# A list scheduler that places relus and output copies itself, counts no latency within an engine, and knows measured load times

## Chip, cores, metric

One core of one Trainium2 chip. The metric is the device time of one execution in microseconds; executions of one kernel mostly agree within 0.3%. The kernel before takes 317.23 us (median of 4 runs, 316.78 to 317.42).

## The reference, cut to what matters

```python
# q, k, v: (4, 8, 768, 64); blocks of 32; mask = neighbours, first and last block, 3 sampled blocks per row block
scores = np.where(mask, scale * np.matmul(q, k.transpose(0, 1, 3, 2)), -1e9)
attn = softmax(scores);  o = np.matmul(attn, v)
x = o.transpose(0, 2, 1, 3).reshape(3072, 512)
h = np.maximum(x @ w_in, 0.0)          # (3072, 2048)
out = (h * h) @ w_out                  # (3072, 512)
```

## The kernel before

While the kernel is built, a list scheduler simulates the five engines with planned durations and emits each task's instructions in the order that it finds. The chip then runs every engine's queue strictly in that order, with semaphores between engines. So the plan decides the order and nothing else; the real times are the chip's.

```python
def ready(self, taken, bufs):                 # earliest planned start of a task
    r = self.after
    for d in self.deps:
        r = max(r, d.end + d.late)            # late: 0.2 us for TensorE's results, 0.08 for VectorE's and ScalarE's
    ...                                       # and the buffers: ps 2, po 1, h 2, y 1 in PSUM
def run_schedule(free, bufs, ring):
    left = {e: [t for t in tasks if t.eng == e] for e in free}
    ...                                       # task that can start first, then smallest key
# --- cut ---
def relu_eng(T, f):                           # fixed: one third, or one half, of the relus on ScalarE
    return "ACT" if (T[0] and f % 3 == 2) or (T[0] == 0 and T[1] and f % 2) else "DVE"
def out_copy(T, ts): ...; nc.scalar.copy(out=ys, in_=py)     # always ScalarE
# --- cut ---
h0, hh = [Task("PE", SQ[w][0] / 2, n_key - half, ...) for half in range(2)]   # hidden product ph: two halves
land_k = [(3.05, 4.3), (5.6,), (8.3,), (11.0,)]              # planned landing of the four head pairs' keys
wu = [Task("PE", 0.107, 1e6, warm_up, ...) for i in range(16)]   # fillers, besides ten at the start
```

TensorE's products are called after what they write: pw warm-ups, pt transposes, pb and pq the mask's products, ps scores, po values (weights times v and row sums), ph hidden, py output. ScalarE makes pT (exponentials) and the inverse of the row sums (ls twice, then rs); VectorE multiplies by the mask and normalises into xT; GpSimd squares.

The softmax here doesn't subtract the row's maximum and nothing guards it: scores larger than these inputs give would overflow.

## Time and profile before

The profiled run took 316.91 us, with a span of 315.2 us in the profile. The prediction shows the profile's lines and sums TensorE's ledger: the distance between starts of successive matmuls, split into the pace of the matmul, 0.096 us for a passage between 64-row or 24-row and 128-row matmuls, and the rest, called a wait. Single waits over 60 ns are put down to what released them. In the first 3.7 us the rest also holds the slow pace of the first warm-ups, some 1.1 us.

### The profile page before, as it was taken

To read this page: it belongs to the slowest core of one execution; us is meant where nothing else is said; L and a number is where in the kernel's file an instruction comes from. 1 tells how busy PE (TensorE), PEld (TensorE's weight loads), DVE (VectorE), ACT (ScalarE), POOL (GpSimd) and SP (SyncE) were. 2 spreads that over 40 slices of the span, in tenths; PEclk is the share of its full clock that TensorE was granted. 3 is DMA by queue.
4 is the path that set the end of the run, shared out by engine and by line. 5 is a ranking of instruction groups with operands and counts; after the bars stand their busy time and mean duration, and the time that the engine had idled before them with its cause. 6 is when DMAs were issued, how large, how long until landed. Compare 5 with 4: busy or idle time off the path is not lost.

```text
span 315.2 us, 6102 instructions
## 1 busy us (share of the span) xinstructions
PE 304.4 (97%) x2303; PEld 171.9 (55%) x2303; DVE 211.2 (67%) x378; ACT 227.3 (72%) x364; POOL 179.2 (57%) x224
## 2 busy tenths in 40 slices
PE   6899999999999989999999999999999999999995
PEld 3565554556656534565565655565555555555542
DVE  7526399785966978979976679776787676332200
ACT  3799999666878999779868888879787886311111
POOL 5560297556875815887756449654544335465620
PEclk9999999999999999999999999999999999999999
DMA  7997369507438355257361075420000000000002
GB/s 223 344 191 150 114 102 199 169 35 200 113 122 235 62 199 177 58 177 196 81 191 35 30 207 128 131 60 33 2 33 35 0 36 34 35 33 33 35 33 100
DMA packets 42597, 34.47 MB, mean 109 GB/s; under 512 B 20680, under 2 KB 39624, under 8 KB 42568
## 3 DMA queue, kind: packets, MB, share of 16 engines
q1 hardware_dynamic: 37656, 29.37, 31.4%
q0 software_dynamic: 4224, 4.19, 8.4%
q10 hardware_dynamic: 688, 0.52, 0.5%
q8 instruction: 18, 0.29, 0.4%
q14 instruction: 11, 0.09, 0.1%
HBM read 27.26 MB, written 6.29 MB: 106 GB/s over the span
## 4 chain that ended last, share of the span: by engine, by line
PE 82%; DVE 7%; ACT 4%; issue 3%; DMA 2%; SPq 1%; DVEq 0%; ACTq 0%
PE ph L434 25%; PE py L464 24%; PE po L397 10%; PE ps L368 10%; PE po L399 9%; DVE pT L379 4%; ACT pT L374 2%; DVE r L445 2%; DMA ks<-in_k_dram 2%; PE ps L364 2%; PE pq L290 1%; SPq L174 1%; DVE qc L305 1%; ACT ls L407 0%; PE pw L217 0%
## 5 line engine op out<-in xcount | busy, mean ns | idle before, releaser
L451 POOL TENSOR_TENSOR g<-r 128x384 bf16<-128x384 f32 (+1 forms) x144 | 131.1, 920 | 103.2 <-DVE r L445 80.4
L374 ACT ACTIVATE pT<-ps 128x1024 bf16<-128x1024 f32 x144 | 142.2, 1020 | 24.8 <-PE ps L368 21.0
L434 PE MATMUL ph<-xT,w_in_sb 128*128 128x384 bf16 (+1 forms) x576 | 119.5, 309 | 1.0 <-DVE r L445 0.4
L464 PE MATMUL py<-w_out_sb,g 128*128 128x512 bf16 x384 | 109.3, 379 | 0.0
L379 DVE TENSOR_TENSOR pT<-pT,mask 128x1024 bf16<-128x1024 bf16 x120 | 98.4, 837 | 15.1 <-ACT pT L374 13.5
L445 DVE TENSOR_SCALAR r<-ph 128x384 f32<-128x384 f32 (+1 forms) x98 | 49.5, 511 | 50.9 <-PE ph L434 40.6
L434 PEld LDWEIGHTS <-w_in_sb 128*128 128x128 bf16 x576 | 53.1, 98 | 46.1 <-issue 12.9
L397 PE MATMUL po<-pT,VA 128*128 128x256 bf16 x288 | 71.2, 274 | 1.9 <-DVE xT L418 1.3
L399 PE MATMUL po<-pT,VB 128*128 128x256 bf16 x288 | 70.7, 272 | 0.0
L368 PE MATMUL ps<-QT,KT 64*128 64x256 bf16 x576 | 50.0, 272 | 0.2 <-ACT pT L374 0.2
L464 PEld LDWEIGHTS <-g 128*128 128x128 bf16 x384 | 36.7, 98 | 24.0 <-issue 2.3
L397 PEld LDWEIGHTS <-VA 128*128 128x128 bf16 x288 | 28.0, 97 | 24.3 <-issue 14.7
L443 ACT ACTIVATE r<-ph 128x384 f32<-128x384 f32 (+1 forms) x46 | 20.8, 451 | 25.7 <-POOL g L451 17.7
L368 PEld LDWEIGHTS <-KT 64*128 64x128 bf16 x576 | 21.4, 94 | 23.2 <-issue 21.2
L399 PEld LDWEIGHTS <-VB 128*128 128x128 bf16 x288 | 28.2, 98 | 7.2 <-issue 0.6
L417 DVE TENSOR_TENSOR xT<-po,rs 64x256 bf16<-64x256 f32 x48 | 19.7, 410 | 12.1 <-ACT rs L408 12.0
L406 ACT ACTIVATE ls<-po 64x256 f32<-64x256 f32 x48 | 18.3, 381 | 12.5 <-PE po L399 11.6
L471 ACT COPY ys<-py 128x512 f32<-128x512 f32 x23 | 13.3, 584 | 13.3 <-PE py L464 13.1
L408 ACT ACTIVATE rs<-ls 128x256 f32<-128x256 f32 x48 | 20.0, 416 | 1.5
L418 DVE TENSOR_TENSOR xT<-po,rs 64x256 bf16<-64x256 f32 x48 | 20.5, 427 | 0.6
L311 POOL CAST VA<-vs 128x384 bf16<-128x384 f32 x16 | 11.5, 719 | 15.7 <-PE po L397 10.4
L407 ACT ACTIVATE ls<-po 64x256 f32<-64x256 f32 x48 | 18.1, 376 | 0.6
(53 smaller groups left out, 108.9 us busy)
## 6 DMA issues: line engine op xcount, KB each, us to landing
vs<-in_v_dram SPq DMA_DIRECT2D x16, 384.0 KB, 4.9
out_dram<-ys SPq DMA_DIRECT2D x23, 256.0 KB, 2.1
ks<-in_k_dram SPq DMA_DIRECT2D x15, 384.0 KB, 4.8
qs<-in_q_dram SPq DMA_DIRECT2D x12, 384.0 KB, 3.5
w_in_sb<-in_moe_w_in_dram POOLq DMA_DIRECT2D x4, 512.0 KB, 8.3
w_out_sb<-in_moe_w_out_dram POOLq DMA_DIRECT2D x4, 512.0 KB, 9.0
qs<-in_q_dram SPq DMA_DIRECT2D x12, 128.0 KB, 5.1
ks<-in_k_dram ACTq DMA_DIRECT2D x1, 256.0 KB, 3.5
```

The lines of the kernel that those rows point to most:

```text
L368: nc.tensor.matmul(ps[:, h, c, :], KT[i][hs, ksl[c]], QT[i][hs, qsl], start=not add, stop=True, skip_group_check=True)
L374: nc.scalar.activation(out=pT, in_=stile.pop((u, qi, cp)), func=AF.Exp, scale=scale)
L379: eng.tensor_mul(out=pT, in0=pT, in1=mask[:, None, qi, cp * 2:cp * 2 + 2, :].broadcast_to([P, 2, 2, QW]))
L397: nc.tensor.matmul(po[:, 0, :], VA[i][:, n, :], pT[:, 0, c, :], start=first, stop=last, skip_group_check=True)
L399: nc.tensor.matmul(po[:, 1, :], VB[i][:, n, :], pT[:, 1, c, :], start=False, stop=last, skip_group_check=True)
L408: nc.scalar.activation(out=rs, in_=ls, func=AF.Exp, scale=-1.0)
L418: V.tensor_mul(out=xT[b][D:P, a, qsl], in0=po[D:P, 1, :], in1=rs[D:P, :])
L434: nc.tensor.matmul(ph, w_in_sb[:, kc, f * P:(f + 1) * P], xT[b][:, kc, c0:c0 + w], start=(kc == 0), stop=(kc == KM - 1))
L443: nc.scalar.activation(out=r, in_=htile.pop((T, f)), func=AF.Relu)
L445: V.tensor_scalar(out=r, in0=htile.pop((T, f)), scalar1=0.0, scalar2=None, op0=AOP.max)
L451: G.tensor_mul(out=g, in0=r, in1=r)
L464: nc.tensor.matmul(py, gtile[T, f][:, ts * P:(ts + 1) * P], w_out_sb[:, f, :], start=(f == 0), stop=(f == NF - 1))
```

## The change

Its intent: relus and copies go to whichever engine is free in the plan; what follows on the same engine needs no semaphore latency; the start is planned with landing times as measured. Core of the diff:

```diff
-                r = max(r, d.end + d.late)
+                r = max(r, d.end + (0 if d.one and d.one == self.one else d.late))
-        left = {e: [t for t in tasks if t.eng == e] for e in free}
+        left = {e: [t for t in tasks if e in t.on] for e in free}
...
-                on = relu_eng(*x)
-                rr = Task(on, SQ[w][1] if on == "DVE" else SQ[w][1] - 0.07, 0, ...
+                rr = Task({"DVE": (SQ[w][1], 0), "ACT": (SQ[w][1] - 0.07, KR)}, 0, 0, ...
-                    yc = Task("ACT", 0.59, 0, ...
+                    yc = Task({"ACT": (0.59, 0), "DVE": (0.59, KY)}, 0, 0, ...          # KR 0, KY 500
...
-    load_part(nc.sync, 0, 0, 0, 1)          # first queries
-    load_part(nc.scalar, 0, 1, 1, CP)       # rest of the first keys
+    load_part(nc.scalar, 0, 0, 0, 1)
+    load_part(nc.sync, 0, 1, 1, CP)
-    V.memset(oh[HALVES[0], :], 1.0)
+    V.memset(oh[HALVES[0], 0:2 * P], 1.0)   # the rest, and GpSimd's selection on it, stand later
-    init_v(V, 0)                            # now on GpSimd with the other three
-    land_k = [(3.05, 4.3), (5.6,), (8.3,), (11.0,)]
+    land_k = [(3.1, 4.7), (6.3,), (9.5,), (12.0,)]      # land_q, land_v likewise
-    wu = [... range(16)]
+    wu = [... range(5)]
-        sc = Task("PE", 0.42 if len(slots) == 1 and s >= N_FIRST else 0.645, ...
+        sc = Task("PE", 0.645 if len(slots) > 1 else 0.56 if s < N_FIRST else 0.42, ...
```

More of the change, by code (lines that the diff above doesn't have):

```diff
@@ L87, in __init__ @@
         def __init__(self, eng, us, key, fn, deps=(), get=None, n=1, put=(), after=0.0, late=0.0, dma=0.0, behind=()):
-            self.eng, self.us, self.key, self.fn = eng, us, key, fn
+            self.on = eng if isinstance(eng, dict) else {eng: (us, key)}
+            self.fn = fn
+            self.one = next(iter(self.on)) if len(self.on) == 1 else None
             self.deps, self.get = list(deps), get
@@ L132, in run_schedule @@
                     at = min(c[0] for c in cand)
-                    t = min((c[1] for c in cand if c[0] <= at + 1e-9), key=lambda t: (t.key, t.order))
+                    t = min((c[1] for c in cand if c[0] <= at + 1e-9), key=lambda t: (t.on[e][1], t.order))
                     if best is None or at < best[0]:
-                        best = (at, t)
+                        best = (at, t, e)
             assert best is not None, "no task can start"
-            at, t = best
-            t.end = t.issued = free[t.eng] = at + t.us * (2 if t.eng == "PE" and at < COLD else 1)
+            at, t, e = best
+            t.end = t.issued = free[e] = at + t.on[e][0] * (2 if e == "PE" and at < COLD else 1)
             if t.dma:
-                t.end = ring[t.eng] = max(ring[t.eng], t.end) + t.dma
+                t.end = ring[e] = max(ring[e], t.end) + t.dma
             if t.get:
@@ L145, in run_schedule @@
                 p.free = max(p.free or 0.0, t.end + t.late)
-            left[t.eng].remove(t)
-            t.fn()
+            for o in t.on:
+                left[o].remove(t)
+            t.fn(e) if len(t.on) > 1 else t.fn()
         return max(free.values())
@@ L245 @@
     make_identity(nc, identb, nomemset=True)
-    one_hot(2, NCH)
     edge = consts.tile([nb, 2], F32, name="edge")
@@ L258 @@
                     op0=AOP.min, op1=AOP.min)
+    V.memset(oh[HALVES[0], 2 * P:], 1.0)
     V.memset(pm[:, 0, 0:1], 0.0)
     V.memset(pm[:, 0, nb - 1:nb], 0.0)
+    one_hot(2, NCH)
     bm = consts.tile([nb, 2, D], BF, name="bm")
@@ L435, in hidden, with relu @@
                              start=(kc == 0), stop=(kc == KM - 1))
-    def relu_eng(T, f):
-        return "ACT" if (T[0] and f % 3 == 2) or (T[0] == 0 and T[1] and f % 2) else "DVE"
-    def relu(T, f):
+    def relu(T, f, on):
         r = work.tile([P, TWM], F32, name="r", tag="r", bufs=R_BUFS)[:, 0:T[2]]
-        if relu_eng(T, f) == "ACT":
+        if on == "ACT":
             nc.scalar.activation(out=r, in_=htile.pop((T, f)), func=AF.Relu)
@@ L465, in output, with out_copy @@
                              start=(f == 0), stop=(f == NF - 1))
-    def out_copy(T, ts):
+    def out_copy(T, ts, on):
         ys = work.tile([P, d_model], F32, name="ys", tag="ys", bufs=3)
@@ L470, in out_copy @@
         ystile[T, ts] = ys
-        nc.scalar.copy(out=ys, in_=py)
+        (nc.scalar.copy if on == "ACT" else V.tensor_copy)(out=ys, in_=py)
     def store(T, ts):
@@ L496 @@
     NQ_Y = 1
-    COLD = 6.5
+    KR, KY = 0, 500
+    COLD = 5.3
     PT_BUFS, R_BUFS, G_BUFS, QC_BUFS = 9, 4, 2 * NF + 3, 5
     K_PARTS = {0: [(0, 1), (1, CP)]}
-    land_k = [(3.05, 4.3), (5.6,), (8.3,), (11.0,)]
-    land_q = [(3.55, 14.6, 16.1), (6.0, 15.0, 16.5), (8.7, 15.4, 16.9), (11.4, 15.8, 17.3)]
-    land_v = [7.2, 9.9, 12.5, 13.7]
+    land_k = [(3.1, 4.7), (6.3,), (9.5,), (12.0,)]
+    land_q = [(3.7, 15.0, 16.5), (6.8, 15.4, 16.9), (9.9, 15.8, 17.3), (12.4, 16.2, 17.7)]
+    land_v = [8.4, 11.0, 13.5, 14.6]
     LAT = 0.08
@@ L517 @@
     wl, tr, gate, mk, tp = {}, {}, [], {}, {HP - 1: []}
-    wu = [Task("PE", 0.107, 1e6, warm_up, get=None if i else "po") for i in range(16)]
+    wu = [Task("PE", 0.107, 1e6, warm_up, get=None if i else "po") for i in range(5)]
     for a, b in zip(wu, wu[1:]):
@@ L524 @@
     oh_t = Task("DVE", 0.2, 0.3, (lambda: one_hot_b(2, NCH)), after=4.2, **SEM)
-    for i in range(1, HP):
-        Task("POOL", 0.8, 0, (lambda i=i: init_v(G, i)), after=4.0 + 2.6 * (i - 1))
+    for i in range(HP):
+        Task("POOL", 0.8, 0, (lambda i=i: init_v(G, i)), after=4.5 + 2.6 * i)
     rc = []
@@ L595, in attend @@
     def attend(s, slots):
-        sc = Task("PE", 0.42 if len(slots) == 1 and s >= N_FIRST else 0.645, s, (lambda: scores(slots)),
+        sc = Task("PE", 0.645 if len(slots) > 1 else 0.56 if s < N_FIRST else 0.42, s, (lambda: scores(slots)),
                   deps=[t for u, qi, cp in slots if qi < NQ_ADD and u < HP for t in (rc[qi], oh_t)[:1 + (cp > 0)]] + [ev[u][1, cp] for u, qi, cp in slots] + [ev[u][0, qi] for u, qi, cp in slots] + sc_all[-1:],
@@ L647 @@
                 hh.deps.append(h0)
-                on = relu_eng(*x)
-                rr = Task(on, SQ[w][1] if on == "DVE" else SQ[w][1] - 0.07, 0, (lambda x=x: relu(*x)), deps=[hh], get="r", put=[h0], **SEM)
+                rr = Task({"DVE": (SQ[w][1], 0), "ACT": (SQ[w][1] - 0.07, KR)}, 0, 0, (lambda on, x=x: relu(*x, on)), deps=[hh], get="r", put=[h0], **SEM)
                 sq_of[x] = Task("POOL", SQ[w][2], n_key, (lambda x=x: square(*x)), deps=[rr], get="g",
@@ L665 @@
                 elif part == NY - 1:
-                    yc = Task("ACT", 0.59, 0, (lambda T_=T_, ts=ts: out_copy(T_, ts)), deps=[yy], get="ys",
+                    yc = Task({"ACT": (0.59, 0), "DVE": (0.59, KY)}, 0, 0, (lambda on, T_=T_, ts=ts: out_copy(T_, ts, on)), deps=[yy], get="ys",
                               put=[yhead], **SEM)
                     Task("SP", 0.5, 0, (lambda T_=T_, ts=ts: store(T_, ts)), deps=[yc], put=[yc], late=2.0)
-    run_schedule({"PE": 3.3, "DVE": 3.8, "ACT": 3.0, "POOL": 4.3, "SP": 10.5},
+    run_schedule({"PE": 3.3, "DVE": 3.9, "ACT": 3.1, "POOL": 4.4, "SP": 10.5},
                  {"ps": 2, "po": 1, "h": 2, "y": 1, "pT": PT_BUFS, "r": R_BUFS, "g": G_BUFS, "ys": 3,
```

## The prediction

> **What bounds the kernel now.** I read the page first, then the table by stretch of time, then TensorE's timeline of the first 17 us and of one busy stretch, then the list of waits. The page's first part:
>
> ```profile
> span 315.2 us, 6102 instructions
> ...
> PE 304.4 (97%) x2303; PEld 171.9 (55%) x2303; DVE 211.2 (67%) x378; ACT 227.3 (72%) x364; POOL 179.2 (57%) x224
> ...
> PE 82%; DVE 7%; ACT 4%; issue 3%; DMA 2%; SPq 1%; DVEq 0%; ACTq 0%
> ```
>
> The first line is the span, the second the busy time of each engine, the third the shares of the chain that ended last. TensorE is the bound in busy time and on the chain; no other engine passes 72%. The table by stretch of time says where that is so:
>
> ```profile
> 0.00:16.00 16.00, 12.19 (x120) 7.22 (x120) 10.38 (x34) 9.37 (x12) 9.28 (x26) 1.00 0.91 283
> 16.00:40.00 24.00, 23.60 (x253) 14.23 (x253) 10.31 (x27) 23.29 (x37) 8.37 (x19) 1.00 0.74 147
> 40.00:150.00 110.00, 107.60 (x837) 60.11 (x836) 90.96 (x153) 90.50 (x148) 75.21 (x90) 1.00 0.58 147
> 150.00:262.00 112.00, 111.69 (x837) 64.93 (x837) 85.06 (x140) 90.69 (x144) 62.00 (x63) 1.00 0.24 70
> ```
>
> The columns are the stretch, its length, then PE, PEld, DVE, ACT, POOL busy, the granted clock, DMA share and GB/s. Before 16 us nobody is full and DMA is at 0.91. From 16 to 40 us ScalarE is full too (23.29 of 24). After 40 us only TensorE is.
>
> "Busy" hides the real pace, so I measured distances between starts of successive matmuls in TensorE's timeline. They repeat to within 2 ns: 109 ns for 256 columns, 162 for 384, 216 for 512, 56 for a 128-column transpose, and two 64-row score matmuls together in 109. A passage between 64-row or 24-row matmuls and 128-row ones costs about 96 ns more, as here:
>
> ```profile
> 40.31 0.27 PE L399 MATMUL po<-pT,VB 128*128 128x256 bf16 x1
> ...
> 40.51 0.39 PE L368 MATMUL ps<-QT,KT 64*128 64x256 bf16 x4
> ...
> 40.84 0.28 PE L397 MATMUL po<-pT,VA 128*128 128x256 bf16 x1
> ...
> 40.96 0.27 PE L399 MATMUL po<-pT,VB 128*128 128x256 bf16 x1
> ```
>
> po to ps takes 0.20 us instead of 0.11; the four score matmuls (two pairs) take 0.33 instead of 0.22.
>
> With these paces TensorE's ledger closes: 1.12 us to the first matmul; 384 x 0.216 (py) + 384 x 0.162 and 192 x 0.109 (ph) + 576 x 0.109 (po) + 336 pairs x 0.109 (ps) + transposes, mask products and 26 warm-ups (2.8) = 273.0; 233 passages x 0.096 = 22.4; waits 14.6; and 4.15 from the last matmul's start to the end of the last store. Sum 315.2. The waits lie 4.6 us before 12 us, 1.6 from 12 to 40, 6.2 from 40 to 150, 2.2 after. So of a span that is 97% busy some 15 us are waiting, 22 us are passages, and the change can touch only these and the warm-ups.
>
> **The start, where most of the waiting is:**
>
> ```profile
> 5.03 0.20 DVE L270 SCALAR_TENSOR_TENSOR bm<-pm 24x48 bf16<-24x48 f32 x1
> ...
> 5.29 0.28 PE L280 MATMUL pb<-oh,bm 24*128 24x256 bf16 x1 [1.08 <-DVE bm L270]
> ...
> 7.46 2.12 ACT L374 ACTIVATE pT<-ps 128x1024 bf16<-128x1024 f32 x2 [1.48 <-PE ps L368]
> ...
> 9.54 0.96 DVE L305 CAST qc<-ks 128x768 bf16<-128x768 f32 x1 [0.90 <-DMA ks<-in_k_dram]
> ...
> 10.56 0.51 PE L317 MATMUL pt<-identb,qc 128*128 128x128 bf16 x6 [1.08 <-DVE qc L305]
> ...
> 11.65 1.02 ACT L374 ACTIVATE pT<-ps 128x1024 bf16<-128x1024 f32 x1 [0.89 <-PE ps L368]
> ...
> 11.67 0.71 PE L217 MATMUL pw<-warm 128*128 128x256 bf16 x5
> ```
>
> The second number is the duration, the bracket the idle time before it and who ended it. The third head pair's keys were planned for 8.3 us and landed at 9.45. TensorE is in order, so it stood on their transposes from 9.3 to 10.56 although the second pair's operands had been evacuated by 8.65. ScalarE then waited 0.89 us, with further idle of 0.28, 0.40 and 0.17 before its next exponentials. The first exponential waited for a VectorE that was busy without a break from 3.9 to 6.6 us.
>
> **What the Trainium skill says.** "TensorEngine Tiling (Array Packing)", section "Key Properties": changing the tiling mode drains TensorE. The trace agrees, with the 96 ns above as its size. "TensorE: Matmul & The Clock Gate", section "Wait — 56ns, not 53.3ns?": warm matmuls start N/2.4 GHz plus about 2.5 ns apart, half that fast when cold. The trace has 216 ns for 512; its first warm-ups stand 0.21 us apart until 3.23 us and later ones 0.11. Same page, "What's actually happening": what warms is some 3.4 us of activity, not a number of matmuls; so I watch whether fewer warm-ups leave the array cold. "DMA: Bandwidth & Descriptors", section "Issuing engines are not separate DMA queues": another issuing engine saves issue time alone. The trace agrees as far as it goes: issues cost 0.43 to 0.49 us on either engine while DMA is 0.91 busy.
>
> **The change part by part.** The scheduler runs while the kernel is built, so I compared the built orders.
> - Warm-ups: 26 become 15. The 11 removed ones stood mostly at 11.67 to 15.14. 11 x 0.109 = 1.2 us of TensorE work, in front of real work that the measured load times now put there.
> - No latency between tasks of one engine: two halves of a hidden product, scores and values now follow each other directly (ph4, po8, ps16 where there were ph2, po4, ps8). Passages fall from 233 to 213: 20 x 0.096 = 1.9 us, all on TensorE.
> - DVE start: the two ones-fills (2 x 0.38) go to POOL, and two thirds of the 0.70 us fill of oh stand later. The chain bm, then row product, moves from 5.03 to about 4.3. The 0.50 us copy of oh now precedes the K evacuation. I put the first exponential at 6.75 instead of 7.46: 0.7 us.
> - Load times and issue order: the bytes are the same, DMA is full, so landings stay within some tenths. But the order is right: scores of the second pair now precede the transposes of the third, and eight value products stand in the wait for its keys, where the first one had stood at 15.48. ScalarE's 1.7 us of idle after the first exponential mostly goes; I leave 0.4 for one wait on the third keys. With the 0.7 ScalarE leads by about 2.2 us at the 25th exponential (40.3 us before), and since it is full from 10 us on, this lead is what TensorE gets. By the 24th score block the new order also holds about 1.3 us more of real TensorE work than the old. So TensorE is 3.5 us ahead at 40 us; this contains the warm-ups and three passages.
> - From 40 us on 17 of the 20 saved passages: 1.6 us.
> - Choice of engine: 98 relus on VectorE and 46 on ScalarE in both orders, only other ones; 6 of 23 output copies go to VectorE. A relu costs 0.556 us against 0.489, so totals hardly move. What counts is TensorE's waits for h buffers: of 6.2 us in single waits over 60 ns after 40 us (24 of them), 3.3 end at a relu, often one behind mask products of 0.84 us, and 1.6 at a normalisation. I take 2 us off, a guess: the choice is made for the planned, not the real, moment.
> - The end (last matmul to last store, 4.15 us) is untouched.
>
> Sum: 3.5 + 1.6 + 2.0 = 7.1 us; 317.36 - 7.1 = 310.3.
>
> **Rivals.** (1) ScalarE keeps the start: it is 23.29 of 24 us full there, and fewer warm-ups are hidden idle anyway. Then only its own lead counts, and if a landing slips (queries now issued behind the first keys) it is 1 us, not 2.2; with no gain in later waits: 317.4 - (1.0 + 1.3 + 1.6) = 313.5. For it: DMA at 0.91 in the first 16 us. Against: its idle there is put down to order, not to bytes, except once. (2) The contiguous products make relus come in pairs on two h buffers, and waits from 40 to 150 us grow from 6.2 to about 9 instead of falling to 4: 317.4 - 5.1 + 3 = 315. For it: ph to ph waits are already the commonest. Against: a half-filled h buffer is no longer held across other work, and both engines may drain it. (3) The plan fits the chip so well that waits after 12 us fall from 10 to 4: 306. For it: from 150 to 262 us they are already only 1.6. (4) The array stays cold for lack of warm-ups: about 1 us lost near 6 us. Twelve warm-ups still fill the stretch to 3.5 us, so I give it little.
>
> **Range and chances.** The passages and warm-ups are counted; the lead at the start may be off by 1.5 us, the later waits by 3 either way. So 310.3, 307.0 to 314.0. Two per cent is 311.0, just above my middle: faster 0.6, same 0.38, slower 0.02.
>
> **What would show it.** Right: first exponential near 6.75 us; no ScalarE idle above 0.5 us from there to 40; the 25th exponential near 38; 213 passages of 96 ns; waits over 60 ns after 40 us near 4 us in sum; last 4.15 us as before. Wrong: key landings later than 9.5 and 12.0; 0.2 us matmul distances after 6 us; TensorE waiting for ps buffers between 13 and 30 us with nothing to fill (then its lead is only ScalarE's); or longer waits for relus in 40 to 150.

## The result, and the profile after

313.87 us (median of 4 runs, 312.81 to 314.40) against 317.23: ratio 0.9892, 95% interval 0.9863 to 0.9921, less than the 2% that would count as faster. The gain is 3.4 us where 7.1 were forecast. The page after (span, busy time, chain):

```profile
span 311.1 us, 6029 instructions
...
PE 297.7 (96%) x2259; PEld 173.3 (56%) x2292; DVE 214.0 (69%) x383; ACT 223.5 (72%) x358; POOL 178.4 (57%) x226
...
PE 79%; DVE 9%; ACT 7%; issue 3%; POOL 1%; DVEq 0%; ACTq 0%
```

TensorE still bounds. It has 2292 weight loads but 2259 matmuls: 33 records are missing, and each leaves a hole of exactly one py, 0.216 us, that is no wait. With those put back the ledger after, from the profiled run (312.81 us), stands against the profiled run before (both have 1.1 us before the first matmul):

| us | pace | passages | waits | after last start | span |
|---|---|---|---|---|---|
| before | 273.0 | 233: 22.4 | 14.6 | 4.15 | 315.2 |
| after | 272.0 | 213: 20.4 | 13.4 | 4.14 | 311.1 |

| waits | 0-12 | 12-16 | 16-40 | 40-100 | 100-150 | 150-262 | 262- |
|---|---|---|---|---|---|---|---|
| before | 4.6 | 0.3 | 1.3 | 3.0 | 3.2 | 1.6 | 0.6 |
| after | 3.7 | 0.1 | 3.4 | 3.1 | 1.3 | 1.9 | 0.0 |

Pace and passages fell by what was counted. Waits before 40 us rose by 1.0 us in sum; after 40 us they fell by 2.2. The table by stretch of the kernel after (stretch, length, PE, PEld, DVE, ACT, POOL busy, granted clock, DMA share, GB/s) shows the same at 16 to 40 us, where TensorE now is busy 21.73 us instead of 23.60:

```profile
0.00:16.00 16.00, 13.11 (x134) 8.59 (x134) 11.57 (x35) 10.13 (x16) 10.31 (x29) 1.00 0.92 283
16.00:40.00 24.00, 21.73 (x233) 13.23 (x230) 10.19 (x24) 22.03 (x34) 9.26 (x19) 1.00 0.73 149
```

The start of the kernel after, in the timeline of all engines (start, duration, engine, what; the bracket is the idle time before it and its releaser; oh is a constant for the mask, bm the small tile from which the mask is made):

```profile
3.19 1.32 POOL L241 TENSOR_SCALAR_AFFINE_SELECT oh<-oh 64x512 bf16<-64x512 bf16 x2 [0.63 <-DVE oh L262]
3.24 0.66 DVE L246 COPY oh<-oh 64x256 bf16<-64x256 bf16 x1
...
3.92 0.67 DVE L270 TENSOR_TENSOR ne<-col,sb_i 24x72 f32<-24x72 int32 x1
...
4.75 0.40 ACT L309 CAST qc<-qs 128x256 bf16<-128x256 f32 x1 [1.20 <-DMA qs<-in_q_dram]
...
4.88 0.20 DVE L274 SCALAR_TENSOR_TENSOR bm<-pm 24x48 bf16<-24x48 f32 x1
...
7.43 1.02 ACT L378 ACTIVATE pT<-ps 128x1024 bf16<-128x1024 f32 x1 [1.60 <-PE ps L372]
...
12.32 1.02 ACT L378 ACTIVATE pT<-ps 128x1024 bf16<-128x1024 f32 x1 [0.84 <-PE ps L372]
```

bm came at 5.08 instead of 5.23 us, not at 4.3; the first queries landed at 4.7 instead of 4.4 us; the first exponential came at 7.43 instead of 7.46. And TensorE's waits from 16 to 48 us, in its timeline:

```profile
18.95 0.40 PE L368 MATMUL ps<-bq,oh 64*128 64x256 bf16 x4 [1.02 <-ACT pT L378]
...
32.17 0.28 PE L401 MATMUL po<-pT,VA 128*128 128x256 bf16 x1 [0.62 <-DVE xT L422]
...
37.10 0.27 PE L401 MATMUL po<-pT,VA 128*128 128x256 bf16 x1 [0.19 <-ACT pT L378]
...
42.02 0.27 PE L401 MATMUL po<-pT,VA 128*128 128x256 bf16 x1 [0.40 <-ACT pT L378]
...
46.64 0.40 PE L372 MATMUL ps<-QT,KT 64*128 64x256 bf16 x4 [0.49 <-ACT pT L378]
```

By distance of starts the first of these waits is 1.09 us. The largest wait of the kernel before between 16 and 40 us is 0.37 us by distance of starts:

```profile
24.33 0.27 PE L397 MATMUL po<-pT,VA 128*128 128x256 bf16 x1 [0.21 <-ACT pT L374]
```

### The profile page after: what moved, and what is told of

It is laid out like the page before. It is cut to its first block, busy times and chain, and to the rows that moved or that the text cites. A ratio compares the mean times of both kernels' runs of the same rounds, so it can differ in the third digit from the quotient of the medians.

```text
span 311.1 us, 6029 instructions
## 1 busy us (share of the span) xinstructions
PE 297.7 (96%) x2259; PEld 173.3 (56%) x2292; DVE 214.0 (69%) x383; ACT 223.5 (72%) x358; POOL 178.4 (57%) x226
## 4 chain that ended last, share of the span: by engine, by line
PE 79%; DVE 9%; ACT 7%; issue 3%; POOL 1%; DVEq 0%; ACTq 0%
PE py L465 24%; PE ph L438 23%; PE po L401 10%; PE ps L372 10%; PE po L403 9%; ACT pT L378 4%; DVE pT L383 3%; DVE r L446 2%; PE ps L368 2%; POOL g L452 1%; ACT ls L411 1%; ACT ls L410 1%; ACT rs L412 1%; DVE xT L422 1%; DVE qc L309 1%
## 5 line engine op out<-in xcount | busy, mean ns | idle before, releaser
L378 ACT ACTIVATE pT<-ps 128x1024 bf16<-128x1024 f32 x144 | 142.2, 1020 | 22.7 <-PE ps L372 22.4
L383 DVE TENSOR_TENSOR pT<-pT,mask 128x1024 bf16<-128x1024 bf16 x120 | 95.8, 809 | 31.7 <-ACT pT L378 29.9
L438 PE MATMUL ph<-xT,w_in_sb 128*128 128x384 bf16 (+1 forms) x576 | 107.3, 309 | 0.2
L465 PE MATMUL py<-w_out_sb,g 128*128 128x512 bf16 x351 | 97.9, 380 | 2.1 <-ACT ys L472 0.5
L446 DVE TENSOR_SCALAR r<-ph 128x384 f32<-128x384 f32 (+1 forms) x98 | 50.2, 513 | 35.5 <-PE ph L438 25.6
L401 PE MATMUL po<-pT,VA 128*128 128x256 bf16 x288 | 68.7, 275 | 2.2 <-DVE pT L383 0.9
L403 PE MATMUL po<-pT,VB 128*128 128x256 bf16 x288 | 68.2, 273 | 0.0
L372 PE MATMUL ps<-QT,KT 64*128 64x256 bf16 x576 | 48.7, 272 | 0.8 <-ACT pT L378 0.5
L372 PEld LDWEIGHTS <-KT 64*128 64x128 bf16 x576 | 22.1, 94 | 25.0 <-issue 20.9
L472 ACT COPY ys<-py 128x512 f32<-128x512 f32 x17 | 9.9, 581 | 28.3 <-PE py L465 28.3
L309 POOL CAST qc<-qs 128x768 bf16<-128x768 f32 (+1 forms) x20 | 15.8, 800 | 3.3 <-PE pt L321 2.3
```

Of the source, the lines that this page charges most:

```text
L372: nc.tensor.matmul(ps[:, h, c, :], KT[i][hs, ksl[c]], QT[i][hs, qsl], start=not add, stop=True, skip_group_check=True)
L378: nc.scalar.activation(out=pT, in_=stile.pop((u, qi, cp)), func=AF.Exp, scale=scale)
L383: eng.tensor_mul(out=pT, in0=pT, in1=mask[:, None, qi, cp * 2:cp * 2 + 2, :].broadcast_to([P, 2, 2, QW]))
L401: nc.tensor.matmul(po[:, 0, :], VA[i][:, n, :], pT[:, 0, c, :], start=first, stop=last, skip_group_check=True)
L403: nc.tensor.matmul(po[:, 1, :], VB[i][:, n, :], pT[:, 1, c, :], start=False, stop=last, skip_group_check=True)
L438: nc.tensor.matmul(ph, w_in_sb[:, kc, f * P:(f + 1) * P], xT[b][:, kc, c0:c0 + w], start=(kc == 0), stop=(kc == KM - 1))
```

## The experiments

Sixteen kernels, timed in several rounds beside the kernel before (four to six runs each). Unless said, the result was correct. There are two questions: which part of the change gives the 3.4 us, and where the 3.0 us forecast before 40 us and not seen went. For the second there are four candidates: ScalarE's load, the late bm and first loads, a cold array, or TensorE's order before its few PSUM buffers. The first four kernels take the change apart; the others take the candidates one by one.

**p1, p2, p3, p4: one part, or all but one.** p1 is the kernel before with only the first pair of lines of the diff; p2 with only the choice of engine; p3 with only the new start (loads, fills, landing times, warm-ups, score time); p4 is the changed kernel with the old start.

> The kernel before with only the rule that a task of one engine sees no latency from another task of that engine (210 passages between 64/24-row and 128-row matmuls instead of 233, 26 warm-ups kept, relus where they were). Theory A (the gain of the change is the denser TensorE order; the new start gave nothing): about 23 x 0.096 = 2.2 us from passages plus up to 1 us of waits, so 314 to 315, ratio 0.991 to 0.994. Theory B (the start gave its part and the later stages gave less than they show): 1 us or less, 316.5.

> The kernel before with only the free choice of VectorE or ScalarE for relus and output copies (233 passages as before; 99 relus on VectorE, 45 on ScalarE; 9 of 23 copies on VectorE). Theory A: waits for relus from 40 to 150 us fall by 1 to 2 us, nothing else, 315.5 to 316.5. Rival: the choice is worth nothing without the latency rule, 317.0 to 317.5.

> The kernel before with only the new start (loads' issue order, oh and ones-fills moved, measured landing times, 15 warm-ups instead of 26, score time 0.56). Theory A: waits of TensorE before 40 us do not fall, and only the warm-ups and 4 passages remain, of which part stood in idle time: 316 to 317.5. Theory B (the start is good and the other two parts spoil 16 to 40 us): 314 to 315, TensorE's waits before 40 us about 4 us instead of 6.2.

> The changed kernel with the start of the kernel before (latency rule and choice kept; 212 passages). Theory A: as fast as the changed kernel or faster, 312.5 to 314. Theory B: slower than the changed kernel by 1 to 2.5 us, 315 to 316.5.

| | us (median) | ratio to before, 95% | passages | waits to 16 / 16-40 / 40-100 / after 100 |
|---|---|---|---|---|
| p1 latency rule | 315.99 | 0.9947, 0.9926 to 0.9967 | 210 | 5.3 / 2.6 / 4.3 / 3.8 |
| p2 choice | 317.02 | 0.9979, 0.9957 to 1.0001 | 233 | 5.9 / 1.8 / 3.1 / 4.5 |
| p3 start | 317.46 | 0.9984, 0.9960 to 1.0008 | 229 | 5.4 / 3.1 / 3.2 / 5.0 |
| p4 rule and choice | 318.89 | 1.0049, 1.0022 to 1.0076 | 212 | 4.9 / 2.6 / 6.1 / 4.7 |

Nearly all the saved passages are the latency rule's (23 of p1, against 4 of p3). The start alone gives nothing that can be told from zero: what 11 warm-ups and 4 passages save comes back as waits from 16 to 40 us. But p4, all but the start, is slower than the kernel before: its order waits 6.1 us between 40 and 100, one wait alone 1.8 us. The parts do not add up (0.995, 0.998 and 0.998 against 0.989 together, and 1.005 for two of them). p1 and p4 fell outside both of their forecasts; p2 took the time that its rival had named (no gain told from zero), and p3 that of its theory A, though TensorE's waits before 40 us did not just stay but rose to 8.5 us. The four profiles also had their first exponential at 8.06 to 8.09 us, 0.6 later than before and after; the next run shows why, and that some 0.9 us of their waits to 16 us belongs to that and not to their orders (4.7 us in the changed kernel run again, 3.8 in the profile above). Parts that do not add up, and this later start, needed runs of their own.

**a2: the changed kernel again.**

> The changed kernel once more, unaltered. If TensorE's clock at 5 to 9 us varies from run to run (full pace in the profiles of the kernels before and after, half pace in those of the four parts), this run lies at 312.8 with a first exponential near 7.4 us when warm, or near 313.5 to 314.2 with one near 8.1 us when cold. If the clock has nothing to do with it, first exponential near 7.4 us again.

313.69 us, runs at 312.79 and at 313.65 to 313.77; ratio 0.9869 (0.9834 to 0.9904). The profiled run (313.73) had its first exponential at 8.07. The first scores in its TensorE timeline, then those of the run shown above:

```profile
7.00 0.61 PE L368 MATMUL ps<-bq,oh 64*128 64x256 bf16 x4
7.40 0.64 PE L372 MATMUL ps<-QT,KT 64*128 64x256 bf16 x4
7.82 0.64 PE L368 MATMUL ps<-bq,oh 64*128 64x256 bf16 x4
```

```profile
6.78 0.39 PE L368 MATMUL ps<-bq,oh 64*128 64x256 bf16 x4
7.00 0.38 PE L372 MATMUL ps<-QT,KT 64*128 64x256 bf16 x4
7.22 0.38 PE L368 MATMUL ps<-bq,oh 64*128 64x256 bf16 x4
```

Four score matmuls start 0.42 us after the four before instead of 0.22: the array is cold, at half pace, though the table by stretch gives a granted clock of 1.00. That agrees with the skill's clock gate page as the prediction cites it; its "What's actually happening" calls the window free-running, which fits one kernel having both states. All of the following must be compared cold with cold or warm with warm.

**w2: five more warm-ups where TensorE waits for bm anyway; b1: the same five in the kernel before.**

```diff
     def rows_product(qi):
         pb = ps_h.tile([P, QW], F32, name="pb", tag="h")
+        for _ in range(5 if qi == 0 else 0):
+            warm_up()
```

> The changed kernel with five more warm-up products directly before the first row product, where TensorE stands from 3.8 to 5.1 us in any case; all else in the same order. Theory (whether the array runs at full pace from 5 to 9 us depends on how busy it was before, and the changed kernel's runs of 312.8 and 313.7 are the two cases): first exponential near 7.4 us in the profile and all runs at 312.6 to 313.0. Rival (the phase alone decides, not the number of warm-ups): again runs at both 312.8 and 313.7, median 313.6.

> The kernel before with the same five warm-up products before the first row product as w2_fill_gap. Theory (only the clock at 5 to 9 us differs between its runs of 316.7 and 317.4): all runs at 316.5 to 316.9, so that the change is worth 3.7 to 4.0 us between warm kernels. Rival: as spread as before, 316.7 to 317.5.

w2: 312.87 us, all four runs within 312.85 to 312.97, ratio 0.9864 (0.9851 to 0.9878), first exponential at 7.44; the interval lies wholly below those of p1 to p4. By the median w2 beats both kernels, the changed one by 0.8 to 1.0 us (a2 and the first measurement), though its interval overlaps theirs. b1: 316.67 (five runs at 316.39 to 316.97, one at 318.88), ratio 0.9983 (0.9955 to 1.0011), so not told from no gain; first exponential at 7.44. All five profiles with extra warm-ups in that gap (w2 and b1, and below s2, m1 and y2) were warm at 7 us, and of the thirteen others three. So warm-ups were too few in both kernels, and by the medians of these two, filled and timed in different rounds, the change is worth 316.67 - 312.87 = 3.8 us. The forecast of 7.1 is not explained by the clock.

**s1, s2: bm before GpSimd's second selection.** s1 moves the second fill of oh and the selection behind bm, and replans. s2 keeps the changed kernel's plan, emits the oh copy behind the first query copy, puts the first queries back on SyncE's queue, and has three extra warm-ups.

```diff
-    V.memset(oh[HALVES[0], 2 * P:], 1.0)      # before the mask arithmetic
-    one_hot(2, NCH)
     ...  bm ...
+    V.memset(oh[HALVES[0], 2 * P:], 1.0)
+    one_hot(2, NCH)
```

> The changed kernel with the second fill of oh and GpSimd's selection on it put behind bm, so that GpSimd works on nothing while VectorE makes bm. Theory (VectorE's copy of oh, 0.66 us against 0.43, and compare, 0.67 against 0.16, were stretched by GpSimd's two selections of 0.66 us beside them): compare back to about 0.16 us, bm done at 4.0 to 4.3 us instead of 5.08, first exponential 0.5 to 0.7 us sooner if the array is equally warm; total 0 to 1 us less. Rival (bm waits for the sampled blocks' load, or the first scores for the first queries landing at 4.7): bm as late, or first exponential unmoved.

> The changed kernel with the plan as it is, but bm made before GpSimd's second selection (as in s1), the oh copy emitted behind the first query copy, the first queries on SyncE's queue again, and three more warm-up products before the first row product to keep the array warm. Theory (the first exponential was to come at 6.75 us and only stayed at 7.43 because GpSimd stretched VectorE's work and the queries landed later): bm done at 3.8, first exponential at 6.5 to 6.9 us. If TensorE's lead counts: total 312.2 to 312.5. Rival (the lead becomes a wait at 9 to 18 us, because third keys and first values are no sooner): first exponential sooner, total 312.8 or more, waits from 8 to 20 us up by as much.

s1 took 315.96 us (0.9945, 0.9909 to 0.9982), with the array cold. Its timeline:

```profile
2.81 0.22 DVE L246 COPY oh<-oh 64x256 bf16<-64x256 bf16 x1
3.07 0.22 DVE L268 TENSOR_TENSOR ne<-col,sb_i 24x72 f32<-24x72 int32 x1
...
3.58 0.20 DVE L272 SCALAR_TENSOR_TENSOR bm<-pm 24x48 bf16<-24x48 f32 x1
...
4.93 0.41 ACT L309 CAST qc<-qs 128x256 bf16<-128x256 f32 x1 [1.36 <-DMA qs<-in_q_dram]
```

With GpSimd idle, copy and compare take 0.22 us each instead of 0.66 and 0.67, and bm is done at 3.78. In the kernel after each ended just behind one of GpSimd's two selections of 0.66 (by 0.05 and 0.08 us). The Trainium skill, "SBUF — State Buffer", section "SBUF: two separate sides", says why: the port pair shared with GpSimd is an exclusive lock held for a whole instruction, and it names VectorE instructions with two SBUF inputs, as the compare has, and those in a 2-port mode among those that are blocked. The trace agrees as far as the ends go. In the kernel before the copy had taken 0.43 us and the compare 0.16. So the 0.76 us of fills that the change took off VectorE came back as 0.74 us of longer copy and compare. The first exponential came at 7.67, 0.4 us sooner than in the changed kernel when cold. The total missed its forecast: it is 2.3 us above a2's, mostly by the new order that moving the selection gives (waits of 4.8 us after 100 against 3.2).

s2, warm, has its first exponential at 6.93 instead of 7.43 us. Total 312.93, ratio 0.9863 (0.9838 to 0.9888): as w2. Its waits moved to the oh copy and the key and query copies between 6.7 and 9.8 us; the 1.09 at 17.7 and all later ones are w2's to 0.1 us. By the 25th exponential nothing is left of the lead: it comes at 42.15, in w2 at 42.10. A first exponential half a microsecond sooner shows no gain here.

**q1: the exchange of the two first loads undone.**

> The changed kernel with only the exchange of the two first loads undone (first queries on SyncE's queue again, rest of the first keys on ScalarE's). Theory: first queries land at 4.3 to 4.5 us instead of 4.7 to 5.0, first exponential up to 0.3 us sooner or the same, total within 0.4 us of the changed kernel. Rival (the exchange is what the faster start rests on): slower by over 0.5 us.

The first queries landed at 4.37, cold first exponential at 8.07 as in a2, 313.49 us (0.9878, 0.9861 to 0.9896). That is within 0.4 us of the changed kernel, as its theory had it: no gain or loss from the exchange shows.

**x1: is it ScalarE?** The prediction let TensorE have ScalarE's lead, because ScalarE is full from 16 to 40 us. If that fullness alone returns the gain as waits, less work on ScalarE should bring it back.

```diff
-        nc.scalar.activation(out=pT, in_=stile.pop((u, qi, cp)), func=AF.Exp, scale=scale)
+        ps = stile.pop((u, qi, cp))
+        if u < HP:                               # first batch: one head only
+            nc.scalar.activation(out=pT[:, 0], in_=ps[:, 0], func=AF.Exp, scale=scale)
+            V.memset(pT[:, 1].rearrange("p c q -> p (c q)").bitcast(F32), 1.00195)
+        else:
+            nc.scalar.activation(out=pT, in_=ps, func=AF.Exp, scale=scale)
```

> Wrong on purpose: the changed kernel with the 36 exponentials of the first batch over one head only (512 instead of 1024 columns on ScalarE), the other head filled with a constant by a short VectorE fill; same order on TensorE. Theory (TensorE's lead of the start is lost because ScalarE is full from 16 to 40 us): TensorE's waits that ScalarE ends (at 17.7, 23.5, 27.5, 36.6, 41.3, 45.9 us, 3.0 us in sum) all but vanish, those that VectorE ends at 30.7 to 31.3 us stay or grow, the 25th exponential comes 3 us or more sooner, total 309.5 to 311.5. Rival (the waits are the order's): the same waits end at others, TensorE's waits from 16 to 48 us stay at 4 us or more, total above 312.5.

313.84 us (0.9894, 0.9880 to 0.9907), cold, where the changed kernel cold is 313.7. The output was wrong. Table by stretch and TensorE's timeline of x1:

```profile
16.00:40.00 24.00, 22.18 (x239) 13.34 (x238) 15.16 (x43) 15.94 (x35) 9.99 (x21) 1.00 0.75 154
```

```profile
19.48 0.40 PE L368 MATMUL ps<-bq,oh 64*128 64x256 bf16 x4 [0.60 <-ACT pT L380]
...
32.49 0.28 PE L406 MATMUL po<-pT,VA 128*128 128x256 bf16 x1 [0.88 <-DVE xT L427]
...
37.46 0.27 PE L406 MATMUL po<-pT,VA 128*128 128x256 bf16 x1 [0.23 <-DVE xT L427]
...
42.26 0.27 PE L406 MATMUL po<-pT,VA 128*128 128x256 bf16 x1 [0.29 <-DVE xT L427]
```

ScalarE is busy 15.94 instead of 22.03 us, yet TensorE's waits from 16 to 70 us are 5.0 us as in the kernel after (2.9 + 2.2 against 3.4 + 1.6), and the 25th exponential comes only 0.6 us sooner than in a2. Between 16 and 48 us the single waits that ScalarE ends did all but vanish (3.0 to 0.7 us), but those that VectorE ends rose from 1.2 to 2.3. Neither text holds as it was put: the theory's gain did not come, and the rival's sign, 4 us or more from 16 to 48 us, failed too (3.5, where the kernel after has 4.8; from 48 to 70 us the waits rose from 0.3 to 1.5). Nor is the run clean. Its fills, 0.27 us each, gave VectorE 9.8 us more to do before 60 us, and at 31, 36 and 41 us one stood just before the normalisation that ends the wait:

```profile
36.17 0.27 DVE L381 MEMSET pT<- 128x256 f32 x1
36.46 0.42 DVE L426 TENSOR_TENSOR xT<-po,rs 64x256 bf16<-64x256 f32 x1
```

So x1 shows that less work on ScalarE, paid for with these fills, bought nothing. It does not show that ScalarE's load is without effect on TensorE.

**i1: the inverse by VectorE reciprocals.** An earlier try at the same question: for the first batch two reciprocals instead of three activations, same plan.

> The changed kernel with the plan as it is, but the 12 inverses of the first batch computed by two VectorE reciprocals instead of three ScalarE activations: 12 x 1.15 us less on ScalarE before about 52 us, of which some 9 us before 42. Theory (TensorE's lead of the start is lost because ScalarE is full from 16 to 40 us): TensorE's waits from 16 to 40 us fall from 3.4 to below 1.5 us, the 25th exponential comes 2 us or more sooner, total 311 to 312.5. Rival (these waits are the order's and VectorE's, such as the 0.78 us for a normalisation at 31 us): waits 3 us or more, total 313.5 to 315, as VectorE only gets more to do.

348.49 us (1.0979), and no answer: a reciprocal of 64x256 took 1.76 us on VectorE, which became the bound, with waits in every stretch to 100 us. Its group of instructions (count, busy time, mean ns, idle before):

```profile
L411 DVE RECIPROCAL rs<-po 64x256 f32<-64x256 f32 x12 | 21.1, 1759 | 7.7 <-PE po L403 7.5
```

**m1, y2: who then?** Both stand on w2, so warm. m1 lets ScalarE write the three mask tiles made from 26 to 31 us; y2 gives the value products of every other head pair a second PSUM buffer in the second query block too.

```diff
+        if qi == NQ_ADD:  nc.scalar.activation(out=dst, in_=mtile.pop((qi, cp)), func=AF.Exp)    # m1
-    NQ_Y = 1
+    NQ_Y = 2                                                                                      # y2
```

> w2_fill_gap with the three mask tiles that are made from 26 to 31 us written by ScalarE (an exponential of 0 or of a large negative number gives the same 1 and 0) instead of VectorE; the same plan and TensorE order. Theory (TensorE's 1.2 us of waits at 30.7 to 31.4 us are VectorE's mask copies of 0.69 us in front of the query copies and the normalisation): these waits fall to 0.5 us or less, total 312.0 to 312.4 against 312.87. Rival (the normalisation is late by its own chain through ScalarE): still 1 us or more there, total 312.8 to 313.5.

> w2_fill_gap with the y buffer used as a second buffer for the value products of every other head pair in the second query block too (as it is in the first). Theory (waits from 16 to 40 us are TensorE standing before the single buffer of the value products until it is normalised): waits from 16 to 40 us 2.0 us or less instead of 3.4, total 311.3 to 312.3, plus or minus 1 for another order behind it. Rival: waits there 3 us or more.

m1: 313.46 us (0.9887, 0.9861 to 0.9913), 0.6 more than w2. The wait went elsewhere, as TensorE's timeline shows:

```profile
32.43 0.38 PE L326 MATMUL pt<-identb,qc 128*128 128x128 bf16 x4 [0.90 <-ACT mask L303]
```

The mask copy now stood in ScalarE's queue behind an inverse. The total lies in the rival's range, but not by the rival's cause: the normalisation was in time (0.19 us of wait), the mask copy was not.

y2: 313.34 us (0.9871, 0.9849 to 0.9893), 0.5 more than w2. The wait at 31 to 32 us for the normalisation is gone, the 25th exponential comes at 39.96 instead of 42.10, and waits from 16 to 70 us are about half a microsecond fewer than in w2; from 16 to 40 us they still come to some 3 us, the rival's sign. In the place of the value products' waits stand scores that wait for a ps buffer:

```profile
31.88 0.40 PE L370 MATMUL ps<-bq,oh 64*128 64x256 bf16 x4 [0.22 <-ACT pT L380]
...
35.86 0.39 PE L370 MATMUL ps<-bq,oh 64*128 64x256 bf16 x4 [0.43 <-ACT pT L380]
...
39.84 0.40 PE L374 MATMUL ps<-QT,KT 64*128 64x256 bf16 x4 [0.32 <-ACT pT L380]
```

So the single buffer is one part of it (half a microsecond, where the theory had 1.4 or more), and the order behind, which waits 0.8 us more from 70 us on, gave it back. With the second buffer every single wait over 60 ns from 16 to 44 us ends at an exponential, and ScalarE has no idle time over 0.15 us from 12.4 to 48 us. This suggests two limits close together, ScalarE's exponentials and the one buffer of the value products: take away one and the other shows. A run that takes away both, x1 with y2, was not made.

**n1, n3: another order from the same planner.** LAT, the planned semaphore latency, is 0.09 or 0.07 instead of 0.08.

> The changed kernel with a planning constant moved without meaning (semaphore latency 0.09 us instead of 0.08), which gives another order (215 passages, 97 relus on VectorE). Theory (what a part of the change gives alone depends on which order it happens to give, as the parts' -1.7, -0.7, -0.2 and together +1.2 suggest): differs from the changed kernel by 1 us or more either way. Rival (orders from one planner are equally good): within 0.5 us of it.

> The changed kernel with the planner's semaphore latency at 0.07 us instead of 0.08: a third order of the same planner (219 passages). Theory (orders of one planner differ by 1 to 2 us by chance): 313 to 317, with 0.6 us for the six more passages and waits after 40 us anywhere from 6 to 9 us. Rival: within 0.6 us of 314.3.

n1: 315.38 us (0.9927, 0.9889 to 0.9965); its profiled run, warm like that of the kernel after, took 314.61 against 312.81, with 1.5 us more waits (70 to 150 us: 4.2 instead of 2.7) and two more passages. n3: 313.48 (0.9882, 0.9864 to 0.9901), although it has six passages more; waits from 70 us on are 4.0 instead of 4.6. One of the two changes of a constant without meaning moved the time by 1.5 to 1.8 us, half of the whole gain; the other hardly moved it.

## Why the prediction was right or wrong

The direction and the bound were right, the size was twice too large. Term by term of its sum:

- **Warm-ups, passages, end: as counted.** Pace fell 1.0 us, passages from 233 to 213 (1.9 us), the end stayed (4.15 and 4.14). p1 shows that the passages come from the latency rule.
- **Waits after 40 us, "I take 2 us off, a guess": 2.2.** Single waits of one hidden product for a relu on VectorE went from 2.4 to 0.4 us, and those of value products for a normalisation from 1.6 to none, while value products waiting for a mask product went from 0.4 to 1.8. The sum fits, by luck in part: it was a guess, and n1, s1 and p4 show that 2 us is also what another order of the same planner can take back.
- **"So TensorE is 3.5 us ahead at 40 us": the step that failed.** Of the 3.5, 1.2 were warm-ups, 0.3 passages, and 2.0 fewer waits. Waits before 40 us went from 6.2 to 7.2: 1.1 less before 16 us, 2.1 more from 16 to 40. The term was 3.0 us too large, and 7.1 - 3.0 is the 4.1 us between the profiled runs; the median gain is 3.4, probably because more of the changed kernel's four runs were cold (only the profiled ones show it).
- **Why, first part: "first exponential at 6.75".** It stayed at 7.43. The freed VectorE time was lost beside GpSimd's selections (s1), and the first queries landed 0.3 us later. s2, which has it at 6.93, shows no gain from it.
- **Why, second part: "With the 0.7 ScalarE leads by about 2.2 us at the 25th exponential", "this lead is what TensorE gets".** The 25th exponential, looked for near 38 us, came at 42.05, 1.7 us later than before (40.32) and not 2.2 sooner. (The lead's own terms, 0.7 + 1.7 - 0.4, give 2.0.) Between the first and the 25th exponential ScalarE is busy 31.7 instead of 30.5 us, with a seventh inverse and two relus now in front of the 25th, and idle 2.9 instead of 2.3: the wait on the third keys was 0.84 and not 0.4 us, and two new ones of 1.06 and 0.47 came at 33.8 and 38.7. The prediction counted the TensorE work that the new order brings forward, 1.3 us, but not the ScalarE work that goes with it. Nor is a lead handed on: s2's first exponential is 0.5 us ahead of w2's, its 25th is not. And a ScalarE that is nearly full did not mean that ScalarE alone sets TensorE's time: with 6 us less of its work from 16 to 40 us TensorE waited as long up to 70 us (x1, with VectorE's fills as its blemish).
- **What the waits from 16 to 40 us are.** In-order TensorE stands before a score until one of two ps buffers is free and before a value product until the one po buffer is normalised. Take one party's work away (x1, m1, y2) and another ends a wait nearby. Why the new orders hit this more (2.6 in p1, 3.1 in p3, 3.4 after, against 1.3) than the old one is not settled: the latency rule and the new start each raise it alone, p2's choice hardly (1.8).
- **Rivals.** (1) had the size nearly right (313.5), by luck: it gave the start 2.3 us and the later waits nothing, where the start gave 0.5 and the later waits 2.2. (2) did not come: waits of 40 to 150 us fell from 6.2 to 4.4. Nor did (3): waits after 12 us hardly moved from 10 (9.8); how its 306 was summed is not told. (4), dismissed with "twelve warm-ups still fill the stretch to 3.5 us", was half of the truth: the array is cold near 7 us in most runs, but of both kernels, so it hardly touches the ratio. By the medians of b1 and w2 it costs 0.6 and 0.8 us, the first not told from zero.

## What to carry to other kernels

Where an in-order engine is nearly full, take its ledger apart by pace, mode passages and waits, and count a saved wait on another engine only if taking that work away moves this one; a full neighbour is no proof that it alone is the bound. When an order brings one engine's work forward, count the neighbour's work that comes with it. A planner's order is one draw: before crediting one part of a change, perturb a constant without meaning and see how far the time moves by itself (here up to 1.8 us in one of two tries, half the gain). Fill a known wait at the start with warm-up matmuls: here every profile with the fill had a warm array, and the changed kernel's median fell by 0.8 us.

## What the Trainium skill lacked or had wrong

- "TensorEngine Tiling (Array Packing)", "Key Properties": says that a change of tiling mode drains TensorE, but gives no size. Here 0.096 us each way, 22.4 us of 315 in the kernel before; also for 24-row matmuls.
- "TensorE: Matmul & The Clock Gate", "What's actually happening": right about the two paces. The page warns ("Seeing it yourself") that a trace's clock events can be unreliable, but no page says that the granted clock in the profile's table can read 1.00 while score pairs start 0.21 us apart instead of 0.11. Nor does one say how long a gap the warming up bears: in the kernels before and after, TensorE has some 2.5 us of warm-ups and then a gap of 1.3 us at most; with three or five more matmuls before the first mask product 5 profiles of 5 were warm, without them 3 of 13.
- "SBUF — State Buffer", "SBUF: two separate sides": what the trace shows fits the lock as stated. The page has a time for a DMA that GpSimd issues while it is locked out, but none for a VectorE instruction. Here a 24x72 compare took 0.67 us instead of 0.22, and a 64x256 copy 0.66 instead of 0.22, beside GpSimd selections of 0.66.
- No page gives the time of a VectorE reciprocal: 1.76 us for 64x256 from PSUM, so that each of the two is longer than all that both replaced, two logarithms and one exponential on ScalarE (1.17 us).
